# Cluster attention and two MLPs on one core: reciprocals in two tiles, and an attention loop put in another order

## The chip, the cores and the metric

The kernel runs on one core of a Trainium2 chip. The metric is the device time of one execution in microseconds. Before the change the median of three runs was 825.31 us (824.75 to 825.86).

## The reference, cut to what matters

Sixteen heads (2 batches of 8), 768 tokens, head size 64. Every query and key is given to the nearest of 16 centroids; a query sees only the keys of its own cluster. Then come two MLPs in a row.

```python
q_assign = argmax(einsum(q_n, c_n)); k_assign = argmax(einsum(k_n, c_n))   # q_n, k_n, c_n: normalised
scores = where(q_assign[:, None] == k_assign[None, :], scale * q @ k.T, -1e9)
attn = exp(scores - max(scores));  attn = attn / (sum(attn) + 1e-9)
x = attn @ v                                  # 1536 tokens x 512 (8 heads x 64)
h = x @ w_in;    x = (h * sigmoid(1.702 h)) @ w_out                 # 2048 wide
g = x @ w_gate;  out = (g * sigmoid(g) * (x @ w_val)) @ w_out2      # 1536 wide
```

Inputs are float32; the weights arrive as 8-byte numbers and are decoded on the chip to float32.

## The kernel before

**Attention.** A loop over 16 heads. The work of head h in the loop has two parts. In the score part, twelve steps (six key blocks of 128, two query halves of 384) run the scores of head h on TensorE (`st`, two matmuls each, L688), and beside each step one product for the row maxima of head h+1 (`smax`, L637). ACT turns each `st` into `p` by an exponential (L698); DVE reduces each `smax` to `nm` (L642). Three PSUM banks hold `st`, so a step can run only three ahead of the exponentials. In the value part `values(h, 0)` to `values(h, 5)` (L742) multiply `p` by `v`. Three of the six blocks of `p` are first split into a high part `ph` (a cast, L705) and a low part `pl` (a subtraction on POOL, L709); five tiles hold `p`. After `values(h, 0)` TensorE turns the maxima into a row (`mrow`), ACT casts it and SP sends it into head h+1's query tile (`q<-row`, L672), which that head's scores need.

**Beside the value part.** ACT and DVE prepare head h+4: `hi_q`, `hi_k` (casts, L441 to L446) and `lo_q`, `lo_k` (subtractions, L450, L456). In odd heads `similar` multiplies queries and keys of heads h+3 and h+4 by the centroids (`sims`, L553) and `largest` finds the best centroid on DVE; in even heads `assign` writes the clusters into the query and key tiles of the next two heads. Six weight blocks are decoded during heads 3 to 8 (`take_in`: two ACT reads, then `joined` and `signed` on DVE, L284 and L289).

**The denominators.** `values` also sums `p` (a column of ones in `v`). `moved(h, n)` copies half n of the result out of PSUM on ACT: for even heads into the tile `xf` with its sums, for odd heads the result into `xf` and the sums' row into a tile `r` (L764). SP sends the sums of a pair of heads to DRAM (`sums`), fetches them spread over the lanes (`rc`), DVE inverts them (`invert`, L779), SP sends them back (`recips`) and fetches them broadcast into the same tile `r` (`r<-recips`, L787), and POOL multiplies `xf` by `r` (`norm_pair`, L792). There is one `r` tile. For the pair of heads 2p and 2p+1, `invert`, `send_recips`, `load_recips` and `norm_pair` all run in head 2p+3. At the end of that same head the next pair's sums are copied into `r`.

**Heads 0 and 1** use another form; `norm(0)` and `norm(1)` (L818 to L820) divide on DVE and free the PSUM bank of `pv`, of which there are two. `norm(1)` stands behind `assign` and `lo_q`, `lo_k` in head 2.

**MLPs.** A planner (`Plan`) lists tasks with an engine, a nominal duration and dependences, and emits them engine by engine in the order of their latest start. `AFTER` is how long it takes a result of an engine to be usable; for SP it stands for a transfer's landing. The work is cut into 28 units: 0 to 7 and 8 to 15 are the first MLP for the two batches, 16 to 27 the second. `DECODES[k]` is how many blocks of the second MLP's weights are decoded beside unit k.

Of the kernel before, what the change touches and what calls it, by code (L numbers as in the profile page):

```python
# [55 lines left out]
class Plan:  # L56
# [6 lines left out]

    AFTER = {"PE": 210.0, "ACT": 80.0, "DVE": 70.0, "POOL": 120.0, "SP": 2200.0}
    SPARE = 120.0
# [119 lines left out]
def tile_cluster_attention_two_mlps(ctx: ExitStack, tc: tile.TileContext, qk, v, cen, w1, w2, wg, wv, w3, out):  # L185
# [116 lines left out]
    def new_a():  # L302
        return dec_p.tile([128, 512], F32, tag="a", name="a")
# [6 lines left out]

    def take_in():

        while True:
            it = items[started[0]]
            fetch_to(started[0] + 1)
            started[0] += 1
            raw = raw_t.pop(it)
            a, t = new_a(), new_t()
            small(a, raw)
            low_bits(t, raw)  # L320
            fetch_to(started[0] + 2)
            yield
            joined(t, a)
            yield
            w = new_wo()
            signed(w, a, t)
            keep(it, w)
            yield

    taking = take_in()  # L330

    def take(n):
        for _ in range(n):
            next(taking, None)

# [130 lines left out]
    load_qk(3)  # L466
    zeros = acst.tile([128, NB], F32R, name="zeros")

# [515 lines left out]
    def beside_block(h, c):  # L984
        if c == 4:
            v_split(h + 1)
        if c == 5:
            moved(h, 0)
        last = h - 1
        if last > 1:  # L990
            if c == 2:
                send_sums(last)
            if last % 2 and c == 4:
                load_sums(last // 2)
        if h % 2 and h > 4:
            hp = (h - 3) // 2
            for at, step in ((0, invert), (0, send_recips), (2, load_recips), (3, norm_pair)):
                if c == at:
                    step(hp)

    for h in range(NH):
# [38 lines left out]
        for c in range(SC) if more else ():  # L1040
# [8 lines left out]
            if c == 0:  # L1049
                load_v(h + 1)  # L1050
                if ahead:
                    if h > 0:
                        if h % 2:
                            hi_k(h + 4)
                        lo_q(h + 4, nc.gpsimd if h == 1 else nc.vector)
                        lo_k(h + 4, nc.gpsimd if h == 1 else nc.vector)
                    if h + 6 < NH:
                        load_qk(h + 6)
# [18 lines left out]
            if h == 1:  # L1077
# [5 lines left out]
                if c == 4:  # L1083
                    do(largest([4, 5], sims + similar([5], ps_s, "s")))
            if h == 2 and c == 0:
                norm(1)
            take(takes.get((h, c), 0))
# [4 lines left out]
            if h % 2 and c == 2 and ahead and h > 1:  # L1092
                do(largest([h + 3, h + 4], similar([h + 3, h + 4], ps_s, "s")))
            if h == 3 and c in (3, 4):
                to_x(0, c - 3)
    send_sums(NH - 2)
    for steps_left in more_steps.values():
# [333 lines left out]
    last_x = rings["xf"].held[1]  # L1431
    for j in range(KC - 2):
        for t0, _ in parts:
            last_x.parts[j, t0] = ([], [])
# [103 lines left out]
    def last_lows():  # L1538
        for c in range(SPLIT):
            by = ("ACT", act(S)) if c == 1 else ("POOL", 1200)  # L1540
            t = p.task(
                *by, lambda c=c: p_high(NH - 1, c, nc.scalar.copy if c == 1 else nc.gpsimd.tensor_copy),
                (), (), exp_tasks[2 * c:2 * c + 2],
            )
            lows.append(p.task("POOL", 1850, lambda c=c: p_low(NH - 1, c), (), (), [t]))
# [25 lines left out]
    def plan_norm(hp, first):  # L1571
        send = p.task("SP", 1000, lambda: (send_sums(NH - 1), load_sums(hp)), (), (), first) if first else None
        turned = p.task("DVE", 350, lambda: invert(hp), (), (), [send] if send else [])
        back = p.task("SP", 1000, lambda: (send_recips(hp), load_recips(hp)), (), (), [turned])
        return p.task(
            "POOL", 1850, lambda: norm_pair(hp), (), [(last_x, (hp % (H // 2), t0)) for t0, _ in parts], [back],
        )

    to_last = [plan_norm(NH // 2 - 2, None), *out_of]
    plan_norm(NH // 2 - 1, out_of)  # L1580
# [77 lines left out]
```

## Time and profile before

| | |
|---|---|
| median of 3 runs | 825.31 us |
| the profiled execution's own time | 825.79 us |
| its span | 823.9 us |
| TensorE busy | 792.8 us (96%) |
| DVE busy | 679.8 us (83%) |
| ACT busy | 513.4 us (62%) |
| POOL busy | 163.9 us (20%) |
| mean granted TensorE clock | 0.981 |

The shares are means over two different stages: attention, up to about 276 us, and the MLPs. The view of waits names for each engine what ended its idle time. The view of windows gives, for each chosen stretch, its length, the busy time of TensorE (and the number of its instructions), of its weight loads (PEld), of DVE, ACT and POOL, then the mean granted clock, the DMA share and GB/s; cut at the first score matmul of each head it gives one row per head.

### The profile page before, as it was taken

The numbers are of one execution on the slowest core, as the hardware profiler recorded it, in microseconds if no ns is written. First come the engines' busy times: TensorE is split into PE (matmuls) and PEld (weight loads), VectorE is DVE, ScalarE is ACT, GpSimd is POOL, SyncE is SP. The second block draws the span as 40 slices with busy tenths as digits, with TensorE's granted clock in tenths as the row PEclk, the third lists the DMA queues.
The fourth block names the chain that finished last, engine by engine and source line by source line (L and its number), as shares of the span: only waits on it lengthen the run. The fifth ranks groups of instructions, "written<-read, shape, count | busy, mean of one in ns | idle before, by whom it ended". The sixth has DMA issues, their size and how long they took to land.

```text
span 823.9 us, 11806 instructions
## 1 busy us (share of the span) xinstructions
PE 792.8 (96%) x4154; PEld 694.0 (84%) x4154; DVE 679.8 (83%) x1224; ACT 513.4 (62%) x881; POOL 163.9 (20%) x155
## 2 busy tenths in 40 slices
PE   8997997898998999999999999999999999999998
PEld 6985676677766789899899999999999999999996
DVE  7885886886887679999999989999877897877753
ACT  7855876785765688788767767666434554443432
POOL 8563434565456600001000000000000000000000
PEclk9998998998998999999999999999999999999999
DMA  5121341311111448778446778464222113321202
GB/s 131 27 83 34 94 132 41 96 47 50 45 24 48 146 132 250 262 239 285 143 152 207 242 263 273 142 215 155 90 78 77 62 42 103 128 63 66 77 1 77
DMA packets 51343, 99.32 MB, mean 121 GB/s; under 512 B 19346, under 2 KB 24806, under 8 KB 51284
## 3 DMA queue, kind: packets, MB, share of 16 engines
q1 hardware_dynamic: 51060, 98.23, 37.6%
q8 instruction: 33, 0.54, 0.3%
q10 hardware_dynamic: 224, 0.33, 0.1%
q14 instruction: 26, 0.21, 0.1%
HBM read 76.75 MB, written 21.06 MB: 119 GB/s over the span
## 4 chain that ended last, share of the span: by engine, by line
PE 70%; DVE 16%; ACT 6%; DMA 3%; issue 3%; POOL 1%; SPq 1%; ACTq 0%; DVEq 0%; POOLq 0%
PE h L384 28%; PE a L384 20%; PE pv L742 8%; PE st L688 7%; PE smax L637 3%; DMA r<-recips 2%; PE pv L801 2%; DVE b L379 2%; DVE t L284 1%; DVE c L1264 1%; DVE wd L289 1%; ACT p L698 1%; DVE g L379 1%; DVE xs L345 1%; DVE s L1208 1%
## 5 line engine op out<-in xcount | busy, mean ns | idle before, releaser
L384 PE MATMUL h<-xc,b 128*128 128x384 f32 x1680 | 317.8, 337 | 1.3 <-DVE c L1264 0.6
L384 PEld LDWEIGHTS h<-xc,b 128*128 128x128 f32 x1680 | 291.6, 188 | 11.8 <-DVE u L1264 2.2
L384 PE MATMUL a<-g,sp 128*128 128x512 f32 (+1 forms) x768 | 144.3, 336 | 0.0
L384 PEld LDWEIGHTS a<-g,sp 128*128 128x128 f32 x768 | 124.9, 188 | 16.9
L642 DVE TENSOR_REDUCE nm<-smax 128x1 f32<-128x384 f32 x192 | 98.6, 553 | 33.5 <-PE smax L637 32.8
L688 PE MATMUL st<-q,k 128*128 128x384 f32 (+1 forms) x384 | 105.4, 367 | 14.6 <-ACT p L698 13.7
L384 PE MATMUL a<-sp,g 128*128 128x512 f32 x432 | 109.6, 393 | 0.0
L698 ACT ACTIVATE p<-st 128x384 f32<-128x384 f32 x192 | 87.1, 491 | 26.0 <-PE st L688 22.3
L688 PEld LDWEIGHTS st<-q,k 128*128 128x128 f32 (+1 forms) x384 | 74.2, 206 | 21.8 <-ACT p L698 20.2
L384 PEld LDWEIGHTS a<-sp,g 128*128 128x128 f32 x432 | 80.2, 188 | 13.2
L376 ACT CAST b<-s 128x512 fp32r<-128x512 f32 x80 | 49.4, 619 | 55.4 <-PE h L384 49.3
L709 POOL TENSOR_TENSOR pl<-p,ph 128x768 fp32r<-128x768 f32 x42 | 77.1, 1843 | 13.1 <-ACT ph L705 10.9
L742 PE MATMUL pv<-p,v 128*65 128x384 f32 x168 | 63.8, 498 | 5.5 <-DVE r L820 5.5
L637 PE MATMUL smax<-k,q 80*128 80x384 f32 x192 | 66.8, 365 | 1.3 <-DVE nm L642 0.9
L1264 DVE TENSOR_TENSOR u<-h,p 128x384 f32<-128x384 f32 x80 | 44.1, 551 | 26.0 <-PE h L384 25.8
L278 ACT ACTIVATE a<-raw 128x512 f32<-128x512 f32 x68 | 45.7, 671 | 26.9 <-DVE wo L289 15.0
L379 DVE TENSOR_TENSOR b<-s,b 128x512 fp32r<-128x512 f32 x80 | 54.6, 684 | 3.7 <-ACT b L376 2.6
L379 DVE TENSOR_TENSOR g<-c,g 128x768 fp32r<-128x768 f32 x56 | 52.1, 952 | 1.7 <-ACT g L376 0.9
L376 ACT CAST g<-c 128x768 fp32r<-128x768 f32 x56 | 44.5, 833 | 11.6 <-DVE c L1279 11.3
L284 DVE SCALAR_TENSOR_TENSOR t<-a,t 128x512 int32<-128x512 int32 x68 | 46.3, 686 | 3.6 <-ACT t L281 3.5
L1272 ACT ACTIVATE c<-c 128x768 f32<-128x768 f32 (+1 forms) x56 | 38.0, 682 | 17.0 <-DVE c L1264 16.6
L376 ACT CAST b<-w 128x768 fp32r<-128x768 f32 x35 | 29.2, 835 | 31.1 <-PE h L384 29.2
(147 smaller groups left out, 1062.5 us busy)
## 6 DMA issues: line engine op xcount, KB each, us to landing
raw<-in_w SPq DMA_DIRECT2D x44, 512.0 KB, 4.6
w<-scr SPq DMA_DIRECT2D x31, 512.0 KB, 3.4
raw<-in_wg SPq DMA_DIRECT2D x12, 512.0 KB, 4.5
raw<-in_wv SPq DMA_DIRECT2D x12, 512.0 KB
w<-scrg SPq DMA_DIRECT2D x12, 512.0 KB, 3.5
w<-scrv SPq DMA_DIRECT2D x12, 512.0 KB, 3.4
st<-in_qk SPq DMA_DIRECT2D x31, 192.0 KB, 3.8
scr<-wd SPq DMA_DIRECT2D x21, 256.0 KB, 6.0
```

The lines of the kernel that those rows point to most:

```text
L278: nc.scalar.activation(a, raw[:, :, 1].bitcast(F32), ACTF.Copy, scale=2.0**-112)
L284: nc.vector.scalar_tensor_tensor(out=t, in0=a.bitcast(I32), scalar=3, in1=t, op0=ALU.logical_shift_left, op1=ALU.bitwise_or)
L376: nc.scalar.copy(to, of)
L379: eng.tensor_tensor(out=to, in0=of, in1=hi.bitcast(F32), op=ALU.subtract)
L384: nc.tensor.matmul(out=out_ps, lhsT=lhs[a], rhs=rhs[b], start=(start and j == 0), stop=(stop and j == 2), skip_group_check=True, **kw)
L637: nc.tensor.matmul(out=ps, lhsT=q2(h)[0:ONE + NC, 1, c * 128:(c + 1) * 128], rhs=k2(h)[0:ONE + NC, 1, n * HALF:(n + 1) * HALF],)
L642: nc.vector.tensor_reduce(out=nm_t[h][:, c, n:n + 1], in_=ps, axis=AX.X, op=ALU.max)
L688: nc.tensor.matmul(out=ps, lhsT=k2(h)[0:rows, a, c * 128:(c + 1) * 128], rhs=q2(h)[0:rows, a, at], start=(a == 0), stop=(a == 1),)
L698: nc.scalar.activation(p_t[h, c][:, n * HALF:(n + 1) * HALF], ps, ACTF.Exp, scale=scale)
L709: nc.gpsimd.tensor_tensor(out=pl_t[h, c], in0=p_t[h, c], in1=ph_t[h, c].bitcast(F32), op=ALU.subtract)
L742: nc.tensor.matmul(out=ps[0:m, 0:HALF], lhsT=w, rhs=x, start=(c == 3), stop=(c == 2 and j == 2), skip_group_check=True,)
L1264: lambda: nc.vector.tensor_tensor(out=to.tile[:, part], in0=ps.tile[:, 0:HALF], in1=other.tile, op=ALU.add),
```

## The change

- Two `r` tiles in turn instead of one (the second in memory freed by taking the warm-up's `zeros` from a query tile not yet in use).
- A pair's transfers are spread. For heads 2p and 2p+1: each head's sums are sent right after its last copy; both are fetched in head 2p+3, inverted there at block 4 and sent at block 5; `r` is fetched in head 2p+4; `norm_pair` runs in head 2p+5, on DVE, behind `largest`. Before, all of this from the inversion on was in head 2p+3, with `norm_pair` on POOL. The last three pairs (10/11 to 14/15) are multiplied on POOL and planned with the MLPs; before, the last two were.
- `v` is fetched two heads ahead, queries and keys are cast five heads ahead.
- `sims` and `largest` of odd heads (from head 5) stand ahead of `values(h, 0)`.
- `ph` of block 1 is cast after step 4 and of block 2 after step 8, both on ACT (block 2 was on POOL).
- `norm(1)` stands ahead of head 3's `mneg`.
- The six early blocks are decoded in heads 5 to 10, two at a time; `DECODES` gives none to units 0 to 7 and four to each of units 8 to 15; SP's `AFTER` is 4000 for 2200.

```diff
-    AFTER = {"PE": 210.0, "ACT": 80.0, "DVE": 70.0, "POOL": 120.0, "SP": 2200.0}
+    AFTER = {"PE": 210.0, "ACT": 80.0, "DVE": 70.0, "POOL": 120.0, "SP": 4000.0}
-    DECODES = (3, 1, 0, 0, 1, 0, 1, 2) + (3, 3, 4, 4, 4, 4, 3, 3)
+    DECODES = (0, 0, 0, 0, 0, 0, 0, 0) + (4, 4, 4, 4, 4, 4, 4, 4)
+    r_tile = in_turn((lambda: r_p[1], 1), (lambda: r_p[0], 1))
     def new_r():
-        return r_p.tile([128, S], F32, tag="r", name="r")
+        return r_tile([128, S], F32, "r")
-    zeros = acst.tile([128, NB], F32R, name="zeros")
+    zeros = q2_t[NQK - 1][:, 0, 0:NB]
-        if i == 6:
-            p_high(h, 1, nc.scalar.copy)
-            p_low(h, 1)
-        if i == 7:
-            p_high(h, 2, nc.gpsimd.tensor_copy)
-            p_low(h, 2)
+        if i in (4, 8):
+            p_high(h, i // 4, nc.scalar.copy)
+            p_low(h, i // 4)
-    takes = {(h, c): n for h in range(3, 9) for c, n in (((1, 1), (2, 2), (4, 1)) if h % 2 else ((1, 1), (3, 1)))}
+    takes = {}
+    for h in range(5, 5 + EARLY_ITEMS, 2):
+        takes.update({(h, 0): (0, 0), (h, 1): (1, 2), (h, 3): (1,), (h + 1, 4): (2,)})
@@ beside_block
-        last = h - 1
-        if last > 1:
-            if c == 2:
-                send_sums(last)
-            if last % 2 and c == 4:
-                load_sums(last // 2)
         if h % 2 and h > 4:
-            hp = (h - 3) // 2
-            for at, step in ((0, invert), (0, send_recips), (2, load_recips), (3, norm_pair)):
+            for at, step in ((4, invert), (5, send_recips)):
                 if c == at:
-                    step(hp)
+                    step((h - 3) // 2)
+            if c == 0 and h > 6:
+                norm_pair((h - 5) // 2, nc.vector)
+        if h % 2 == 0 and h > 5:
+            if c == 1:
+                load_recips((h - 4) // 2)
@@ the loop over heads
             moved(h - 1, 1)
+            send_sums(h - 1)
+            if h % 2 and 4 < h < NH - 1:
+                load_sums((h - 3) // 2)
+        if h == 2:
+            norm(1)
         if 1 < h < NH - 1:
             mneg(h + 1)
+            if h % 2 and ahead and h > 3:
+                do(largest([h + 3, h + 4], similar([h + 3, h + 4], ps_s, "s")))
+            for part in takes.get((h, 0), ()):
+                take(part)
             values(h, 0)
             mrow(h + 1)
-        if ahead and h > 0:
-            hi_q(h + 4)
-            if h % 2 == 0:
-                hi_k(h + 4)
+        if h > 1 and h + 2 < NH:
+            load_v(h + 2)
+        if h + 6 < NH and h > 1:
+            load_qk(h + 6)
+        casts = [] if not h else [h + 4] if h < 3 else [7, 8] if h == 3 else [h + 5] if h + 5 < NH else []
+        if casts and h != 1:
+            hi_q(casts[0])
+            hi_k(casts[0])
...
@@ last pairs
-    to_last = [plan_norm(NH // 2 - 2, None), *out_of]
+    to_last = [plan_norm(NH // 2 - 3, []), plan_norm(NH // 2 - 2, []), *out_of]
```

**How it moves instructions.** POOL from the low parts of head 5 to those of head 6, before; `ph`, `pl` are parts of `p`, `vh`, `vl` of `v`:

```order
L705 CAST ph<-p 128x768
L709 TENSOR_TENSOR pl<-p,ph 128x768 x2
L705 CAST ph<-p 128x768
L709 TENSOR_TENSOR pl<-p,ph 128x768
L792 TENSOR_TENSOR xf<-xf,r 128x768
L713 CAST vh_189<-v_186 128x3x64
```

The same place after:

```order
L706 CAST ph<-p 128x768
L710 TENSOR_TENSOR pl<-p,ph 128x768 x3
L714 CAST vh_192<-v_189 128x3x64
```

The multiplication by `r` and one cast per head have left POOL.

DVE in head 7, from the last maxima on, before (`rc` are the sums of a pair, `T`, `U` and `mx` belong to `largest`, `t` and `wo` to the decoding):

```order
L653 TENSOR_REDUCE nr<-nm 128x6
L779 TENSOR_SCALAR rc<-rc 128x12
L780 RECIPROCAL rc<-rc 128x12
L450 TENSOR_TENSOR q_1_184<-st_196,q_1_184 64x768
L456 TENSOR_TENSOR k_1_185<-st_196,k_1_185 64x768
L284 SCALAR_TENSOR_TENSOR t<-a,t 128x512
L289 SCALAR_TENSOR_TENSOR wo<-a,t 128x512
L577 STREAM_TRANSPOSE T<-sims 128x384
```

After, from the end of `largest` on:

```order
L593 TENSOR_TENSOR T<-T,wd 128x384
L790 TENSOR_TENSOR xf<-xf,r 128x768
L286 SCALAR_TENSOR_TENSOR t<-a,t 128x512
L291 SCALAR_TENSOR_TENSOR wo<-a,t 128x512
L451 TENSOR_TENSOR q_2_179<-st_196,q_2_179 64x768
L457 TENSOR_TENSOR k_2_180<-st_196,k_2_180 64x768
L286 SCALAR_TENSOR_TENSOR t<-a,t 128x512
L777 TENSOR_SCALAR rc<-rc 128x12
L778 RECIPROCAL rc<-rc 128x12
L643 TENSOR_REDUCE nm<-smax 128x1 x12
```

`largest` now comes first, the multiplication by `r` follows it, and the inversion has gone from the front of the row to its end.

DVE in head 2 (`rd` and `r` are `norm(1)`), before:

```order
L642 TENSOR_REDUCE nm<-smax 128x1 x12
L653 TENSOR_REDUCE nr<-nm 128x6
L601 TENSOR_REDUCE mx_941<-T 128x24
L603 TENSOR_TENSOR T<-T,mx_941 128x384
L606 TENSOR_SCALAR T<-T,s_246,s_247 128x384
L610 STREAM_TRANSPOSE oT<-T 64x384 x2
L450 TENSOR_TENSOR q_1_184<-st_195,q_1_184 64x768
L456 TENSOR_TENSOR k_1_185<-st_195,k_1_185 64x768
L818 TENSOR_SCALAR rd<-pv 128x6
L819 RECIPROCAL rd<-rd 128x6
L820 TENSOR_TENSOR r<-pv,rd 128x6x64
```

And after:

```order
L643 TENSOR_REDUCE nm<-smax 128x1 x12
L816 TENSOR_SCALAR rd<-pv 128x6
L817 RECIPROCAL rd<-rd 128x6
L818 TENSOR_TENSOR r<-pv,rd 128x6x64
L654 TENSOR_REDUCE nr<-nm 128x6
```

`norm(1)` has moved past the whole of `assign` and the two subtractions, to stand ahead of `nr`, from which the row of maxima is made.

## Rows read from the trace of the kernel before

**Rows 1.** The page: its first line.
```profile
span 823.9 us, 11806 instructions
```

**Rows 2.** Windows: heads 2, 3, 4, 6, 9, 13; sum of heads 2 to 14.
```profile
52.20:74.63 22.43, 16.79 (x69) 11.34 (x69) 14.35 (x26) 11.73 (x20) 8.01 (x7) 0.85 0.23 69
74.63:90.97 16.34, 16.03 (x82) 12.42 (x82) 11.82 (x21) 13.23 (x25) 8.36 (x7) 1.00 0.27 83
90.97:105.14 14.17, 13.94 (x68) 10.30 (x68) 13.62 (x25) 13.02 (x24) 7.07 (x5) 1.00 0.16 45
...
121.84:143.09 21.25, 16.20 (x68) 12.90 (x68) 13.62 (x24) 13.57 (x24) 9.76 (x8) 0.84 0.18 55
...
176.65:192.34 15.69, 15.38 (x77) 11.76 (x77) 12.88 (x26) 11.30 (x21) 7.94 (x7) 1.00 0.46 115
...
242.58:256.94 14.36, 13.98 (x69) 10.31 (x68) 13.39 (x20) 8.88 (x20) 8.51 (x7) 1.00 0.34 92
...
sum 223.92, PE 201.23 PEld 152.46 DVE 175.39 ACT 156.07 POOL 114.43; mean PE 15.48 PEld 11.73 DVE 13.49 ACT 12.01 POOL 8.80
```

**Rows 3.** Waits of PE, first 300 us: total, times, longest.
```profile
PE st L688 <- ACT p L698: 13.7, 6, 5.1
PE pv L742 <- DVE r L820: 5.5, 1, 5.5
PE sims L553 <- DVE k L456: 1.7, 6, 0.4
```

**Rows 4.** The chain that ended last, heads 5 to 6: start, length, what.
```profile
118.94 5.80 DMA r<-recips
...
125.77 1.81 POOL xf L792
...
127.60 0.48 ACT r L764
...
128.64 1.01 PE st L688 x2
```

**Rows 5.** Timeline of DVE, head 2: start, length.
```profile
66.34 0.15 DVE L818 TENSOR_SCALAR rd<-pv 128x6 f32<-128x6 f32 x1
...
66.75 0.56 DVE L820 TENSOR_TENSOR r<-pv,rd 128x384 f32<-128x384 f32 x1
```

**Rows 6.** Windows: head 4's value part; head 9's score part and value part.
```profile
98.08:105.14 7.06, 7.06 (x32) 4.12 (x31) 6.85 (x11) 6.66 (x11) 2.88 (x3) 1.00 0.05 10
176.65:183.41 6.76, 6.63 (x38) 6.28 (x38) 6.00 (x12) 5.83 (x13) 4.98 (x5) 1.00 0.47 122
183.41:192.34 8.93, 8.75 (x41) 5.49 (x40) 6.88 (x15) 5.47 (x9) 2.96 (x3) 1.00 0.45 110
```

**Rows 7.** DVE by line and shape, heads 2 to 14: busy, mean ns.
```profile
L289 DVE SCALAR_TENSOR_TENSOR wo<-a,t 128x512 int32<-128x512 int32 x6 | 4.4, 738 | 0.2
...
L590 DVE TENSOR_TENSOR T<-T,mx 128x384 f32<-128x384 f32 x6 | 3.3, 558 | 0.2
L379 DVE TENSOR_TENSOR xc<-xf,xc 128x768 fp32r<-128x768 f32 x3 | 2.9, 955 | 3.9 <-ACT xc L376 3.9
```

**Rows 8.** Timeline, heads 4 and 5.
```profile
99.22 1.82 POOL L709 TENSOR_TENSOR pl<-p,ph 128x768 fp32r<-128x768 f32 x1
...
99.53 1.93 DVE L603 TENSOR_TENSOR T<-T,mx 128x384 f32<-128x384 f32 x1
...
108.11 0.35 POOL L713 CAST vh<-v 128x192 fp32r<-128x192 f32 x1 [7.08 <-DMA v<-in_v]
```

**Rows 9.** Timeline of ACT, head 3: the cast of `ph`.
```profile
78.94 0.84 ACT L705 CAST ph<-p 128x768 fp32r<-128x768 f32 x1
```

**Rows 10.** Windows: the MLPs in three stretches.
```profile
300.00:440.00 140.00, 139.20 (x787) 128.48 (x786) 137.02 (x241) 110.84 (x191) 2.43 (x1) 1.00 0.69 224
440.00:580.00 140.00, 139.84 (x794) 130.60 (x793) 131.59 (x231) 96.48 (x160) 0.00 (x0) 1.00 0.63 212
580.00:820.00 240.00, 240.00 (x1236) 220.05 (x1235) 182.41 (x325) 98.00 (x156) 0.00 (x0) 1.00 0.21 71
```

More of the change, by code (lines that the diff above doesn't have):

```diff
@@ L309, in new_wo, with take @@
         return wo_p.tile([128, 512], F32, tag="wo", name="wo")
[L311 to L316, printed above, removed]
+    taken = {}
+    def take(part):
+        n = started[part]
+        it = items[n]
+        started[part] += 1
+        if part == 0:
+            fetch_to(n + 1)
             raw = raw_t.pop(it)
-            a, t = new_a(), new_t()
+            a, t = taken[n] = new_a(), new_t()
             small(a, raw)
             low_bits(t, raw)
-            fetch_to(started[0] + 2)
-            yield
+            fetch_to(n + 3)
+        elif part == 1:
+            a, t = taken[n]
             joined(t, a)
-            yield
+        else:
+            a, t = taken.pop(n)
             w = new_wo()
@@ L327, in take_in @@
             keep(it, w)
[L328 to L334, printed above, removed]
     ctx.enter_context(
@@ L1049, in tile_cluster_attention_two_mlps @@
             if c == 0:
-                load_v(h + 1)
-                if ahead:
[L1052 to L1058, printed above, removed]
+                if h < 2:
+                    load_v(h + 1)
+                    if h:
+                        load_v(h + 2)
+                        hi_k(casts[0])
+                    for i in casts:
+                        lo_q(i, nc.gpsimd)
+                        lo_k(i, nc.gpsimd)
+                    load_qk(h + 6)
+                if ahead:
                     if h + 5 == NH:
@@ L1084, in tile_cluster_attention_two_mlps @@
                     do(largest([4, 5], sims + similar([5], ps_s, "s")))
-            if h == 2 and c == 0:
-                norm(1)
-            take(takes.get((h, c), 0))
+            for part in takes.get((h, c), ()) if c else ():
+                take(part)
+            if h > 1 and c == 1:
+                for i in casts[:1]:
+                    lo_q(i)
+                    lo_k(i)
             for n in beside_values.get((h, c), ()):
@@ L1091, in tile_cluster_attention_two_mlps @@
                 fetch_to(2)
-            if h % 2 and c == 2 and ahead and h > 1:
-                do(largest([h + 3, h + 4], similar([h + 3, h + 4], ps_s, "s")))
+            if h == 3 and c == 4:
+                do(largest([6, 7], similar([6, 7], ps_s, "s")))
+                hi_q(8)
+                hi_k(8)
+            if h == 4 and c == 2:
+                lo_q(8)
+                lo_k(8)
             if h == 3 and c in (3, 4):
                 to_x(0, c - 3)
-    send_sums(NH - 2)
     for steps_left in more_steps.values():
@@ L1431, in tile_cluster_attention_two_mlps @@
     last_x = rings["xf"].held[1]
-    for j in range(KC - 2):
+    for j in range(KC - 3):
         for t0, _ in parts:
@@ L1539, in last_lows @@
         for c in range(SPLIT):
-            by = ("ACT", act(S)) if c == 1 else ("POOL", 1200)
+            by = ("ACT", act(S)) if c else ("POOL", 850)
             t = p.task(
-                *by, lambda c=c: p_high(NH - 1, c, nc.scalar.copy if c == 1 else nc.gpsimd.tensor_copy),
+                *by, lambda c=c: p_high(NH - 1, c, nc.scalar.copy if c else nc.gpsimd.tensor_copy),
                 (), (), exp_tasks[2 * c:2 * c + 2],
@@ L1571, in plan_norm @@
     def plan_norm(hp, first):
-        send = p.task("SP", 1000, lambda: (send_sums(NH - 1), load_sums(hp)), (), (), first) if first else None
-        turned = p.task("DVE", 350, lambda: invert(hp), (), (), [send] if send else [])
-        back = p.task("SP", 1000, lambda: (send_recips(hp), load_recips(hp)), (), (), [turned])
+        if hp > NH // 2 - 3:
+            if first:
+                first = [p.task("SP", 1000, lambda: send_sums(NH - 1), (), (), first)]
+            got = p.task("SP", 1000, lambda: load_sums(hp), (), (), first)
+            turned = p.task("DVE", 350, lambda: invert(hp), (), (), [got])
+            first = [p.task("SP", 1000, lambda: (send_recips(hp), load_recips(hp)), (), (), [turned])]
         return p.task(
-            "POOL", 1850, lambda: norm_pair(hp), (), [(last_x, (hp % (H // 2), t0)) for t0, _ in parts], [back],
+            "POOL", 1850, lambda: norm_pair(hp), (), [(last_x, (hp % (H // 2), t0)) for t0, _ in parts], first,
         )
-    to_last = [plan_norm(NH // 2 - 2, None), *out_of]
+    to_last = [plan_norm(NH // 2 - 3, []), plan_norm(NH // 2 - 2, []), *out_of]
     plan_norm(NH // 2 - 1, out_of)
```

9 lines of the change are left out of this document (6 added, 3 removed).

## The prediction, made before the changed kernel had run

> **What bounds the kernel now.** I read the page's first line, then the view of windows, first by stage and then by head, then the waits of TensorE, and last the chain that ended last around one such wait. The profiled execution took 825.79 us, of which the span is 823.9 us [rows 1]; what lies around the span, 1.89 us, stays. The median of the runs is 825.31 us, 0.48 us lower, so I sum on 825.79 and take 0.48 off at the end.
>
> From 300 us on TensorE is the bound: in the three stretches of the MLPs it is busy 139.20 of 140, 139.84 of 140 and 240.00 of 240 us [rows 10]. Nothing is to be won there. Heads 2 to 14 are different: they take 223.92 us, in which TensorE is busy 201.23 [rows 2], and some of that busy time ran at half clock. Head 4 takes 14.17 us at granted clock 1.00, head 6, which has the same work, 21.25 us at 0.84; head 2 takes 22.43 us at 0.85 [rows 2]. Odd heads that also multiply by the centroids take 15.69 us where nothing disturbs them (head 9) [rows 2].
>
> What disturbs them is named by the waits: `st` waits 13.7 us in all for the exponentials (6 times, up to 5.1), and `pv` once 5.5 us for `norm(1)` [rows 3]. The chain before the longest of these shows why [rows 4]: `r` takes 5.80 us to come back from DRAM, POOL then multiplies for 1.81 us, then ACT copies a row of sums into `r` (0.48 us), and only then come the exponentials and the score matmul at 128.64. The copy has to wait because there is one `r` tile and POOL is still reading the pair before. ACT works in order, so the exponentials of head 6 queue behind the copy. Around such a wait the clock is granted at the lower of its two levels, 1.2 of 2.4 GHz, for a part of the head, which is how the mean comes to 0.84 in head 6. So a wait of about 5 us costs 7: 21.25 less 14.17 is 7.08.
>
> **The change part by part.**
>
> *Two `r` tiles, `norm_pair` two heads later.* The copy in head 2p+3 goes into the other tile. That tile was last read by the multiplication of pair p-1, which now stands in the same head on DVE, behind `largest`. The multiplication ends some 12 us after the head's start: 6.76 us of scores [rows 6], half a microsecond for the last maximum, seven operations of `largest` at about 0.56 [rows 7], and its own 0.96. The copy comes at some 14.5 us, as it needs five of the six groups of values: 6.76, 1.87 for `sims` (8.93 less 7.06) and five sixths of 7.06 [rows 6]. So this wait goes, and the half clock with it. The transfers now have a head each, over 13 us against a landing of 5.80 us at worst [rows 4], so they are late nowhere. The price is 0.96 us of DVE (the nearest row is a two-input operation on the same 128x768, 955 ns) [rows 7]. Heads 7, 9, 11 and 13 have that on DVE, and heads 5, 7 and 9 one more decoding step (0.74 us) [rows 7]. Head 9 has DVE busy 12.88 of 15.69 us [rows 2], so 14.6 afterwards, still less than the head. What hides it is TensorE's value part; should it stop doing so, it costs at most 0.96 us in four heads.
>
> *The `norm(1)` of head 2.* It moves ahead of `nr`, so the 5.5 us wait goes. In its place `nr`, and with it the row of maxima, comes later by `norm(1)`'s own length: from 66.34 to 66.75 + 0.56, that is 0.97 us [rows 5]. TensorE waits that long for `mrow`, from nothing (if the last maximum leaves DVE early) to 0.97; I take 0.97.
>
> *`sims` first.* The same matmuls, moved ahead of the values. Their inputs were cast a head earlier, so the wait for the low part of `k`, 1.7 us in 6 times [rows 3], goes. New is that their PSUM banks are those of `st`: the first must wait for the exponential of step 9. That is between nothing and one step, 0.56 us (6.76 / 12) [rows 6]; I take nothing beyond what the value below leaves for it.
>
> *`v` two heads ahead.* POOL sat 7.08 us until `v` landed and began `vh` only after the head had begun [rows 8]; its three subtractions then ended late. They end earlier now, which frees the tiles of `p` that step 10 of the same head waits for.
>
> *`ph` on ACT.* One cast of 0.84 us [rows 9] per head moves from POOL to ACT, into the score part, where ACT is busy 5.83 of 6.76 us [rows 6]: 6.67 of 6.76. That fits, barely. Ends: nothing, or the full 0.84 us in 13 heads, 10.9 us. I take nothing, since the casts stand after steps 4 and 8, each with room for the three PSUM banks to run ahead, where one cast stood before at step 6 and cost part of a step anyway.
>
> *Weight decoding.* Units 8 to 15 get 32 blocks for 28, and 0 to 7 none for 8. A block is two DVE operations of about 0.7 us (the one shown is 738 ns) [rows 7]. Four blocks more in 440 to 580 us are 5.9 us at most: DVE goes from 131.59 to 137.5 of 140, which is what it has now in 300 to 440 (137.02), where TensorE loses 0.80 us against 0.16 [rows 10]. So this costs up to 0.6 us, and the first stretch, 11.8 us lighter on DVE, gives back up to 0.8. The new landing time for SP only reorders. I take 0.5 us for both, between a gain of 0.8 and a loss of 3.
>
> **The sum.** An even head is 14.17 us at most (head 4) [rows 2]. Its parts at their cleanest are 6.76 us (a score part with no long wait, of head 9) and 7.06 us (the value part of head 4) [rows 6], 13.82 together. I take 14.0, between these, for heads 4, 6, 8, 10, 12, 14 and for 13, which has no `sims` either. An odd head with `sims` took 6.76 + 8.93 = 15.69 us [rows 6] including some 0.4 us of the wait for `k`; I take 15.4 for heads 5, 7, 9 and 11. Head 3 stays at 16.34 [rows 2]. Head 2 is 14.17 + 0.97 = 15.14. Together 7 x 14.0 + 4 x 15.4 + 16.34 + 15.14 = 191.1 us for 223.92, a gain of 32.8. Then 825.79 - 32.8 + 0.5 - 0.48 = 793.0 us. With every head at its cleanest (13.82, and 15.3) it would be 1.7 us less, and without the 0.97 us and with the first MLP stretch clean 789.0; with 14.17 and 15.69 it is 795.4.
>
> **The rivals.**
>
> *ACT becomes the bound of the score part.* For it: 6.67 of 6.76 us leaves nothing for the copies of the head before, which fall into the same part. Against it: busy times in a part paced by TensorE contain the latency of each exponential, not only the time until the next can start. Half of the 0.84 us in 13 heads, 5.5 us, gives 798.5; all of it 803.9.
>
> *POOL and DVE hold each other up.* A comparison on DVE of 128x384 takes 558 ns where `largest` does it [rows 7], and 1.93 us where `assign` does it at 99.53, while POOL is at a `pl` from 99.22 to 101.04 [rows 8]. If the four multiplications and the subtractions beside them wait so for a `pl` of 1.82 us, four odd heads lose up to 1.8 us each: 7.2 us, 800.2. Against it: `pl` now ends, by my count, some 8 us into the head and the multiplication begins after 11. Beside this row stands the Trainium skill, Perfetto Trace Analysis, section Optimizing Scalar/DVE Operations: GPSIMD and DVE share a read port of SBUF, so moving work from one to the other may not help. It speaks against this very move; the row agrees that such waits exist, and by the rule the four multiplications would be dear whenever POOL reads at that time.
>
> *The `r` tile is still waited for.* If DVE's multiplication slips behind the copy (a margin of about 2.5 us), ACT waits again in heads 5 to 13. With half of the gain of those heads lost (223.92 less 191.1, without head 2's 7.3, is 25.5) it is 805.8. The margin speaks against it, since the wait would have to be longer than in any row for DVE.
>
> *Slower: the decoding starves TensorE.* In units 8 to 15 each block's two DVE operations stand in one row with the sums that release TensorE's PSUM banks. If the planner's new order puts the blocks ahead of them and none of the 32 is hidden, 32 x 1.48 = 47 us are added in these units: 793.0 + 47 = 840. It decides against the change from 32 us on, that is when TensorE's busy share between 410 and 550 us falls below 81% (139.84 of 140 + 32). Against it: 28 blocks stand there now at 139.84 of 140 us [rows 10].
>
> **How the numbers follow.** The forecast of 793.0 us with its own range of 789 to 797 has a chance of 0.72. ACT as the bound 0.14, POOL and DVE 0.05, the `r` tile 0.06, starved MLPs 0.03. The range that should hold 8 in 10 takes the forecast's and the nearer half of ACT's: 788.5 to 800.5. A measurement of this kernel can tell about 0.2% (1.7 us) from no change. All cases but the last are faster by more; of the last I give two thirds to slower. Faster 0.96, same 0.02, slower 0.02.
>
> **What would show it.** Right: in the waits of TensorE the lines for the exponentials and for `norm(1)` fall from 19.2 us to under 3, ACT's copy into `r` waits for nobody, the granted clock is 1.00 in all heads, even heads take 13.8 to 14.2 us, and the MLPs are as long as before (within 1 us). Wrong: a score part over 7 us with ACT busy throughout (first rival), long `xf` or `q` operations on DVE beside a `pl` (second), a wait of ACT for DVE's `xf` (third), TensorE under 99% in units 8 to 15 (fourth). A wait for the row of maxima at the start of heads 6 and 8, where two fetches of 512 KB now stand ahead of it on SP's queue, would be one I have left out.

## The result, and the profile after

The changed kernel takes 789.86 us (median of 4 runs, 788.83 to 790.90), the kernel before 825.19 us on the same chip (4 runs): a ratio of 0.9571 (95% interval 0.9555 to 0.9588). The profiled execution took 788.83 us with a span of 787.0 us. A second profile of the same kernel (changed_again, below) gives heads 2 to 14 in 189.27 us where the first gives 189.36, and the rest in 545.57 for 545.33. Over the eight traces with the same quotas and landing time (table below) the rest spreads over 0.9 us, so half a microsecond can be read in the heads but not in the rest. The profiled execution of one kernel below (old_ph_no_norm, 948.73 us) ran at a mean granted clock of 0.753 from end to end, and that kernel's numbers are those of its other three executions.

The view of windows by head (columns as in [rows 2]): heads 2, 3, 4, 7, 8, 11, 12 and the sum of heads 2 to 14.

```profile
52.31:67.00 14.69, 14.19 (x69) 10.32 (x69) 13.08 (x26) 12.12 (x21) 7.21 (x6) 1.00 0.33 102
67.00:82.85 15.85, 15.78 (x83) 12.48 (x83) 10.28 (x19) 13.95 (x25) 7.18 (x6) 1.00 0.14 38
82.85:97.07 14.22, 13.91 (x69) 10.29 (x69) 13.48 (x25) 13.96 (x27) 7.62 (x6) 1.00 0.19 48
...
126.48:141.86 15.38, 15.31 (x77) 11.76 (x76) 13.91 (x25) 13.67 (x26) 7.21 (x6) 1.00 0.51 137
141.86:155.59 13.73, 13.63 (x69) 10.34 (x69) 12.44 (x25) 12.83 (x23) 7.64 (x6) 1.00 0.32 83
...
184.72:200.85 16.13, 15.51 (x76) 11.72 (x76) 14.02 (x27) 9.70 (x21) 7.50 (x6) 1.00 0.16 44
200.85:214.44 13.59, 13.59 (x68) 10.34 (x68) 10.86 (x20) 11.06 (x22) 7.64 (x6) 1.00 0.14 33
...
sum 189.36, PE 187.45 PEld 142.25 DVE 165.96 ACT 161.38 POOL 98.20; mean PE 14.42 PEld 10.94 DVE 12.77 ACT 12.41 POOL 7.55
```

These heads took 223.92 us before [rows 2], so 34.6 us went here. Of it 13.8 us is TensorE's busy time (201.23 to 187.45) and 20.8 us is its idle time (22.7 to 1.9). Of the busy time 11.8 us went in the five heads 2, 6, 8, 10 and 14, whose granted clock had been 0.82 to 0.90; it is now 1.00 in every head.

TensorE's waits from 60 us to the end (columns as in [rows 3]):

```profile
PE smax L638 <- DVE nm L643: 0.6, 1, 0.6
PE h L384 <- DVE c L1285: 0.3, 1, 0.3
PE mrow L670 <- DVE nr L654: 0.3, 1, 0.3
PE st L689 <- ACT p L699: 0.2, 1, 0.2
```

Of the 13.7 and 5.5 us of [rows 3] 0.2 us is left. The largest wait is a new one, for the first maxima of head 11, and the row of maxima of head 2 is waited for 0.3 us.

The other 2.45 us (1.7 to 2.6 over the eight traces) came from the stage behind head 14. One window from the start of head 15 to the end, first of the kernel before, then of the changed one:

```profile
276.12:823.90 547.78, 542.98 (x2935) 498.65 (x2934) 462.80 (x813) 321.65 (x537) 12.16 (x9) 1.00 0.45 149
```

```profile
241.67:787.00 545.33, 541.41 (x2935) 498.62 (x2934) 463.34 (x813) 322.65 (x538) 12.19 (x7) 1.00 0.45 149
```

The number of instructions is the same; 0.88 us of the gain is TensorE's idle time and 1.57 us its busy time. Split at the same instruction of TensorE, about the 800th, first before, then changed:

```profile
276.12:421.96 145.84, 144.71 (x804) 131.02 (x804) 131.18 (x227) 113.32 (x198) 12.16 (x9) 1.00 0.66 213
```

```profile
241.67:385.27 143.60, 143.27 (x804) 131.01 (x804) 129.79 (x222) 106.89 (x186) 12.19 (x7) 1.00 0.59 186
```

So 2.24 us are won up to there, and what follows takes 401.73 us for 401.94. Last, the timeline of DVE and of POOL from the middle of head 7 (which starts at 126.48) into head 8 (141.86):

```profile
134.88 0.36 DVE L581 TENSOR_TENSOR T<-T 128x192 f32<-128x192 f32 x1
...
137.82 0.95 DVE L790 TENSOR_TENSOR xf<-xf,r 128x768 f32<-128x768 f32 x1
...
142.68 0.17 DVE L777 TENSOR_SCALAR rc<-rc 128x12 f32<-128x12 f32 x1
142.88 0.23 DVE L778 RECIPROCAL rc<-rc 128x12 f32<-128x12 f32 x1
143.02 3.77 DVE L643 TENSOR_REDUCE nm<-smax 128x1 f32<-128x384 f32 x8
...
132.90 1.85 POOL L710 TENSOR_TENSOR pl<-p,ph 128x768 fp32r<-128x768 f32 x1 [0.22 <-ACT ph L706]
...
135.11 0.60 POOL L715 TENSOR_TENSOR vl<-v,vh 128x192 fp32r<-128x192 f32 x1
143.49 0.83 POOL L706 CAST ph<-p 128x768 fp32r<-128x768 f32 x1 [7.78 <-ACT p L699]
```

The two engines nearly take turns. POOL's third low part ends at 134.75, 0.13 us before DVE's first addition of `largest`; POOL is through with `v` at 135.71, two microseconds before DVE multiplies; and DVE's last operation on SBUF ends at 143.11, 0.38 us before POOL begins again. The experiments show that this order in time carries a good part of the gain.

### The profile page after: what moved, and what is told of

Same layout as the page of the kernel before. It is cut to its first block, busy times and chain, and to the rows that moved or that the text cites. A ratio compares the mean times of both kernels' runs of the same rounds, so it can differ in the third digit from the quotient of the medians.

```text
span 787.0 us, 11774 instructions
## 1 busy us (share of the span) xinstructions
PE 777.6 (99%) x4154; PEld 683.8 (87%) x4154; DVE 671.0 (85%) x1228; ACT 519.7 (66%) x895; POOL 147.7 (19%) x137
## 4 chain that ended last, share of the span: by engine, by line
PE 89%; DVE 5%; ACT 4%; issue 1%; DVEq 0%; ACTq 0%
PE h L384 35%; PE a L384 29%; PE pv L740 11%; PE st L689 7%; PE smax L638 3%; PE pv L799 2%; ACT p L699 2%; PE sims L554 1%; ACT ph L706 1%; DVE nm L643 1%; DVE b L379 1%; PE warm L474 0%; DVE s L1229 0%; ACT q L442 0%; DVE wo L291 0%
## 5 line engine op out<-in xcount | busy, mean ns | idle before, releaser
L689 PE MATMUL st<-q,k 128*128 128x384 f32 (+1 forms) x384 | 98.0, 345 | 1.0 <-ACT p L699 0.2
L699 ACT ACTIVATE p<-st 128x384 f32<-128x384 f32 x192 | 84.4, 492 | 18.2 <-PE st L689 16.4
L689 PEld LDWEIGHTS st<-q,k 128*128 128x128 f32 (+1 forms) x384 | 68.2, 190 | 8.0 <-ACT p L699 6.1
L638 PE MATMUL smax<-k,q 80*128 80x384 f32 x192 | 62.8, 344 | 1.1 <-DVE nm L643 0.6
L740 PE MATMUL pv<-p,v 128*65 128x384 f32 x168 | 61.9, 485 | 0.0
L376 ACT CAST g<-c 128x768 fp32r<-128x768 f32 x56 | 45.3, 835 | 12.2 <-DVE c L1300 11.8
```

Of the source, the lines that this page charges most:

```text
L376: nc.scalar.copy(to, of)
L638: nc.tensor.matmul(out=ps, lhsT=q2(h)[0:ONE + NC, 1, c * 128:(c + 1) * 128], rhs=k2(h)[0:ONE + NC, 1, n * HALF:(n + 1) * HALF],)
L689: nc.tensor.matmul(out=ps, lhsT=k2(h)[0:rows, a, c * 128:(c + 1) * 128], rhs=q2(h)[0:rows, a, at], start=(a == 0), stop=(a == 1),)
L699: nc.scalar.activation(p_t[h, c][:, n * HALF:(n + 1) * HALF], ps, ACTF.Exp, scale=scale)
L740: nc.tensor.matmul(out=ps[0:m, 0:HALF], lhsT=w, rhs=x, start=(c == 3), stop=(c == 2 and j == 2), skip_group_check=True,)
```

## Experiments

The table puts all of them beside each other. "Heads" is the sum of heads 2 to 14, "rest" the time from the start of head 15 to the end of the span, both of the profiled execution. Each ratio is to the kernel before run beside it (medians from 823.15 to 825.19 us).

| kernel | median (range), us | ratio to before (95%) | heads | rest |
|---|---|---|---|---|
| before | 825.19 (824.75 to 825.86) | | 223.92 | 547.78 |
| changed | 789.86 (788.83 to 790.90) | 0.9571 (0.9555 to 0.9588) | 189.36 | 545.33 |
| changed_again | 789.21 (788.82 to 790.01) | 0.9571 (0.9544 to 0.9598) | 189.27 | 545.57 |
| two_r_only | 811.39 (807.46 to 813.10) | 0.9841 (0.9809 to 0.9874) | 205.51 | 547.85 |
| two_r_norm1 | 806.52 (800.57 to 807.41) | 0.9791 (0.9768 to 0.9813) | 197.89 | 548.49 |
| old_quotas | 791.85 (791.24 to 792.31) | 0.9611 (0.9592 to 0.9629) | 189.15 | 548.58 |
| old_landing | 790.85 (789.83 to 791.69) | 0.9598 (0.9579 to 0.9618) | 189.02 | 546.56 |
| norm_on_pool | 791.48 (790.91 to 792.02) | 0.9605 (0.9566 to 0.9643) | 191.89 | 545.94 |
| old_ph | 801.20 (800.78 to 803.10) | 0.9727 (0.9686 to 0.9768) | 203.00 | 545.23 |
| sims_late | 802.16 (796.97 to 805.91) | 0.9738 (0.9668 to 0.9808) | 200.34 | 545.35 |
| v_one_ahead | 793.44 (792.34 to 795.51) | 0.9631 (0.9590 to 0.9673) | 195.43 | 545.92 |
| old_ph_no_norm | 791.91 (791.82 to 791.97) | 0.9601 (0.9570 to 0.9633) | | |
| ph_both_late | 797.10 (796.51 to 797.54) | 0.9664 (0.9637 to 0.9691) | 196.29 | 546.11 |
| x0_later | 788.27 (787.70 to 789.38) | 0.9560 (0.9536 to 0.9584) | 188.31 | 545.87 |

### The r tile alone: two_r_only

The kernel before with

```diff
-    r_p = pool(ctx, "r", 1)
+    r_p = [pool(ctx, "r0", 1)]
...
+    r_tile = in_turn((lambda: r_p[1], 1), (lambda: r_p[0], 1))
...
-        return r_p.tile([128, S], F32, tag="r", name="r")
+        return r_tile([128, S], F32, "r")
...
+    r_p.append(pool(att, "r1", 1))
...
-    zeros = acst.tile([128, NB], F32R, name="zeros")
+    zeros = q2_t[NQK - 1][:, 0, 0:NB]
```

> The kernel before with two r tiles in turn (and zeros in a query tile, which makes the room), all else in its old order: the multiplication by r stays on POOL in head 2p+3, behind the transfers. Theory (one r tile makes ACT's copy, and behind it the exponentials, wait): TensorE's waits for p fall from 13.7 us to under 2, the granted clock is 1.00 from head 3 on, head 6 takes 14.2 us for 21.25, and of the 26 us that heads 3 to 14 lost against the changed kernel at least 20 are won: 800 to 805 us. Rival (POOL's row): the multiplication still stands up to 5.8 us at the front of POOL's row, ahead of ph and pl of the next head; TensorE then waits for pl in place of p, at least half of the loss stays, and the time is 812 us or more.

811.39 us. Heads 3 to 14 fall from 201.49 to 184.16 us, by 17.3 of the 26.8 us that the whole change wins in them. This trace is of the shortest of four executions (807.46 us); by the medians the second tile is worth 12.1 us (823.48, the kernel before beside it, less 811.39). TensorE's wait for `p` at `st` falls from 13.7 to 0.5 us (with 1.8 us at `pv` instead). So the theory names a large part, but the rest stays, and neither number that was expected came (800 to 805; 812 or more). Head 6 and head 12 from the windows, and ACT's wait for POOL between 60 and 260 us:

```profile
120.82:136.99 16.17, 14.35 (x68) 10.18 (x68) 15.59 (x24) 12.57 (x23) 10.12 (x8) 1.00 0.25 80
...
212.81:229.56 16.75, 15.19 (x68) 11.89 (x68) 12.82 (x20) 10.16 (x20) 10.96 (x8) 0.90 0.03 6
```

```profile
ACT p L701 <- POOL pl L712: 4.6, 4, 3.2
```

The rival was right that POOL's row is a cause of its own: the multiplication waits for its transfer at the front of that row, the low parts come late, and the exponential of step 10 gets no tile (the lines are under two_r_norm1).

### With norm(1) moved as well: two_r_norm1

```diff
+        if h == 2:
+            norm(1)
         if 1 < h < NH - 1:
             mneg(h + 1)
...
-            if h == 2 and c == 0:
-                norm(1)
```

> The kernel before with two r tiles and with norm(1) ahead of head 3's row of maxima, all else as before. The difference to two_r_only prices norm(1). Theory (the 5.5 us wait and the half clock it brings are one loss): head 2 takes 14.7 us for 22.43, so 7 to 7.7 us less than two_r_only. Rival (the half clock in head 2 has another cause, the way out of heads 0 and 1): only the wait itself goes, 4.5 to 5.5 us less, and head 2 still shows a granted clock under 0.95.

Head 2 takes 14.68 us at a granted clock of 1.00, where two_r_only has 21.35 at 0.92: the wait and the half clock are one loss, as the theory said. In the two traces the heads differ by 7.62 us, the medians by 4.9 (the profiled execution was the shortest of five); what the other four lost elsewhere is open. The trace also shows what the rest of the change has to remove. First head 6 (POOL, then ACT), then head 12 (DVE, POOL, and TensorE's wait):

```profile
117.74 1.83 POOL L795 TENSOR_TENSOR xf<-xf,r 128x768 f32<-128x768 f32 x1 [9.55 <-DMA r<-recips]
...
123.23 0.87 ACT L701 ACTIVATE p<-st 128x384 f32<-128x384 f32 x2 [3.00 <-POOL pl L712]
...
205.13 2.60 DVE L347 TENSOR_TENSOR xs<-xf 128x768 f32<-128x768 f32 x1
...
205.01 1.91 POOL L795 TENSOR_TENSOR xf<-xf,r 128x768 f32<-128x768 f32 x1 [5.53 <-DMA r<-recips]
...
209.32 0.44 PE L640 MATMUL smax<-k,q 80*128 80x384 f32 x1 [1.76 <-DVE nm L645]
```

In head 6 a late transfer becomes a late low part. In head 12 there is another effect: DVE's subtraction takes 2.60 us (0.93 in the changed kernel) while POOL multiplies beside it, the maxima queue behind it, TensorE waits 1.76 us and runs at a mean granted clock of 0.90 in that head.

### The planner's numbers: old_quotas and old_landing

```diff
-    DECODES = (0, 0, 0, 0, 0, 0, 0, 0) + (4, 4, 4, 4, 4, 4, 4, 4)
+    DECODES = (3, 1, 0, 0, 1, 0, 1, 2) + (3, 3, 4, 4, 4, 4, 3, 3)
```

> The changed kernel with DECODES of before. Theory (the MLPs are 2.45 us shorter because units 0 to 7 no longer decode): the 2.2 us are given back in units 0 to 7, 791.8 to 792.3 us, with TensorE's three waits there back. Rival (SP's landing time of 4000 in the planner did it): no change, 789.6 to 790.2 us. Third: what stands at the border of the two stages did it: no change here nor with the old landing time.

```diff
-    AFTER = {"PE": 210.0, "ACT": 80.0, "DVE": 70.0, "POOL": 120.0, "SP": 4000.0}
+    AFTER = {"PE": 210.0, "ACT": 80.0, "DVE": 70.0, "POOL": 120.0, "SP": 2200.0}
```

> The changed kernel with SP's AFTER at 2200 as before. Theory (quotas): no change, 789.6 to 790.2 us. Rival (landing time): 791.8 to 792.3 us. Third: no change.

With the old quotas the rest takes 548.58 us, 3.25 more than in the changed kernel (2.5 to 3.4 over the eight traces), and TensorE waits in the first units again, 2.2 us in three places for DVE (in the kernel before 0.9 us in three places, one of them for ACT; in the changed kernel 0.3 us in one):

```profile
PE h L384 <- DVE c L1285: 2.2, 3, 1.6
```

So the quotas give the gain. Of the 3.25 us 1.9 is idle time and 1.4 busy time of TensorE. The old landing time gives 546.56 us; the eight traces with the new quotas and landing time (table) lie between 545.23 and 546.11, so it may cost a few tenths, which these runs do not settle. The ratios agree: that of old_quotas lies above the changed kernel's interval (though it touches the wider one of changed_again), that of old_landing overlaps it.

### One part of the attention loop taken back at a time

norm_on_pool:

```diff
-                norm_pair((h - 5) // 2, nc.vector)
+                norm_pair((h - 5) // 2)
```

> The changed kernel with norm_pair of the four pairs in heads 7 to 13 on POOL in place of DVE, at the same place in the program (r has landed a head earlier, so POOL waits for nothing). Theory (the gain comes from the second r tile and the late place, not from the engine): POOL has room, 7.2 of 15.4 us busy, the multiplications run some 8 to 10 us into the head, TensorE waits for nothing new: 789 to 791 us. Rival (POOL's reading holds DVE up, as its xs of 2.60 us for 0.96 beside POOL's xf in two_r_norm1 suggests): largest runs beside POOL's xf, up to 1.8 us late in each of four heads, the maxima of the next head wait: 792 to 797 us.

791.48 us lies between the two ranges. The heads take 2.53 us more, and it is heads 8 and 10 that lose (15.14 and 15.12 us for 13.73 and 13.78). The rival is right in the place it named, and costs less than it said. DVE and POOL in head 7, TensorE in head 8:

```profile
134.43 1.86 DVE L581 TENSOR_TENSOR T<-T 128x192 f32<-128x192 f32 x1
...
134.25 1.83 POOL L790 TENSOR_TENSOR xf<-xf,r 128x768 f32<-128x768 f32 x1
...
144.62 0.44 PE L638 MATMUL smax<-k,q 80*128 80x384 f32 x1 [1.13 <-DVE nm L643]
```

An addition that takes 0.36 us alone ends at 136.29, 0.21 us after POOL's multiplication has ended at 136.08: it is not slowed but held. DVE does 0.95 us less and is nevertheless later.

old_ph:

```diff
-        if i in (4, 8):
-            p_high(h, i // 4, nc.scalar.copy)
-            p_low(h, i // 4)
+        if i == 6:
+            p_high(h, 1, nc.scalar.copy)
+            p_low(h, 1)
+        if i == 7:
+            p_high(h, 2, nc.gpsimd.tensor_copy)
+            p_low(h, 2)
```

> The changed kernel with the casts of ph where they stood: block 1 on ACT after step 6, block 2 on POOL after step 7. Theory (ACT's room was what decides, and both places fit): POOL ends its low parts 0.8 to 1.7 us later in each head, still ahead of the values that need them: 789 to 791 us. Rival (POOL's low parts are what step 10 waits for, as in head 6 of two_r_norm1 with 3.00 us): the exponential of step 10 waits for pl in some of 13 heads, 0.3 to 0.8 us each: 793 to 800 us.

801.20 us, 13.6 us more in the heads. The theory fell, and the rival had the wrong wait: `st` waits 0.9 us for `p`, but `smax` 7.7 us for `nm`. Head 8 (windows), then POOL and DVE in heads 7 and 8, and TensorE's longest wait:

```profile
143.28:163.14 19.86, 16.52 (x69) 13.22 (x68) 16.82 (x26) 12.89 (x22) 8.66 (x7) 0.83 0.23 58
```

```profile
135.96 1.83 POOL L710 TENSOR_TENSOR pl<-p,ph 128x768 fp32r<-128x768 f32 x1
...
145.82 2.13 POOL L710 TENSOR_TENSOR pl<-p,ph 128x768 fp32r<-128x768 f32 x1
...
136.32 1.69 DVE L581 TENSOR_TENSOR T<-T 128x192 f32<-128x192 f32 x1
...
145.04 1.25 DVE L286 SCALAR_TENSOR_TENSOR t<-a,t 128x512 int32<-128x512 int32 x1
146.21 1.77 DVE L780 TENSOR_SCALAR rc<-rc 128x12 f32<-128x12 f32 x1
...
148.71 0.69 PE L638 MATMUL smax<-k,q 80*128 80x384 f32 x1 [3.34 <-DVE nm L643]
```

The third low part ends later, holds an operation of `largest`, and DVE's row no longer ends before POOL starts in the next head. There the rest of it is held again: an operation on 12 columns takes 1.77 us for 0.17. The first maxima are 3.34 us late, and the clock falls behind them.

old_ph_no_norm tests that this is the path:

```diff
             if c == 0 and h > 6:
-                norm_pair((h - 5) // 2, nc.vector)
+                r_t.pop((h - 5) // 2)
```

> As old_ph, but the multiplications by r of the four pairs in heads 7 to 13 are left out (the result of these pairs stays undivided), so DVE has 0.95 us less to do in each of these heads. Theory (old_ph is slow because DVE's last operations of odd heads run past the next head's start into POOL's ph and pl, where they are stretched, and the maxima come late): DVE is through before POOL starts there, t and rc take 0.69 and 0.17 us again for 1.25 and 1.77, heads 8 and 10 fall from 19.86 and 19.44 to 14 to 15.5 us, and the time is 791 to 794 us. Rival (the late low parts themselves make TensorE wait): no change beyond 1 us, 800 to 802 us.

791.91 us. Taking 0.95 us from DVE in four heads gives back 9.3 us, though POOL's casts and low parts stand where they stood in old_ph. The theory holds in the time; the lengths of `t` and `rc` and of heads 8 and 10 that it names could not be read.

ph_both_late separates the engine from the place:

```diff
-        if i in (4, 8):
-            p_high(h, i // 4, nc.scalar.copy)
-            p_low(h, i // 4)
+        if i in (6, 7):
+            p_high(h, i - 5, nc.scalar.copy)
+            p_low(h, i - 5)
```

> The changed kernel with the two casts of ph on ACT both, but after steps 6 and 7, so that only the engine of block 2 differs from old_ph, and only the place from the changed kernel. POOL's third pl then ends some 8.9 us into a head, between 8.3 (changed kernel) and 9.7 (old_ph). Theory (where pl ends decides, since DVE's largest begins at 7.8 to 8.3 us into an odd head): one operation of largest is stretched by 0.5 to 0.8 us, 790 to 795 us. Rival (the place after steps 4 and 8 is what matters, for the exponentials): TensorE waits for p, 796 us or more.

797.10 us: the rival. TensorE's waits, and the operation of `largest` that the theory had in view:

```profile
PE st L689 <- ACT p L699: 4.6, 16, 0.3
```

```profile
137.97 0.50 DVE L581 TENSOR_TENSOR T<-T 128x192 f32<-128x192 f32 x1
```

DVE is held for 0.14 us only. TensorE now waits for `p` in short pieces, and each head from 2 to 14 loses 0.2 to 0.7 us; that two casts in a row use up what the three banks of `st` let ACT fall behind fits this and is not shown apart.

sims_late:

```diff
-            if h % 2 and ahead and h > 3:
-                do(largest([h + 3, h + 4], similar([h + 3, h + 4], ps_s, "s")))
...
+            if h % 2 and ahead and h > 3 and c == 2:
+                do(largest([h + 3, h + 4], similar([h + 3, h + 4], ps_s, "s")))
```

> The changed kernel with sims and largest of odd heads from 5 on back behind the third group of values, the casts still five heads ahead. Theory as predicted (sims first removes the wait for k): TensorE's wait for k comes back, 0.3 to 0.4 us in four heads, 791 to 792 us. Rival A (the earlier casts already removed it, k is ready a head before): no wait for k, 789 to 791 us. Rival B (largest now runs into the next head's maxima): TensorE waits for nm in heads 6 to 12, 0.5 to 1.5 us each with the clock falling behind it, 793 us or more.

802.16 us, 11.0 us more in the heads: rival B, and more than it said. No wait for `k` comes back. TensorE's waits up to 300 us, then POOL and DVE in head 8, which starts at 143.31:

```profile
PE smax L638 <- DVE nm L643: 9.3, 4, 3.5
```

```profile
146.00 2.13 POOL L710 TENSOR_TENSOR pl<-p,ph 128x768 fp32r<-128x768 f32 x1
...
146.39 1.76 DVE L777 TENSOR_SCALAR rc<-rc 128x12 f32<-128x12 f32 x1
```

v_one_ahead:

```diff
-        if h > 1 and h + 2 < NH:
-            load_v(h + 2)
...
+                load_v(h + 1)
                 if h < 2:
-                    load_v(h + 1)
                     if h:
-                        load_v(h + 2)
```

> The changed kernel with v fetched one head ahead, at block 0, as before. Theory as predicted (a late v holds up POOL, whose low parts then end late and free p for step 10 late): POOL's vh waits for DMA v in some heads, pl ends up to 1 us later, and TensorE waits for p now and then: 790 to 794 us. Rival (v lands within the head even so, with POOL's row free of the multiplication): no change, 789 to 791 us.

793.44 us, 6.1 us more in the heads of a profiled execution that was the longest of four (795.51). Head 10 starts at 172.36; POOL, ACT and TensorE:

```profile
172.60 0.34 POOL L714 CAST vh<-v 128x192 fp32r<-128x192 f32 x1 [5.95 <-DMA v<-in_v]
...
172.98 2.02 ACT L699 ACTIVATE p<-st 128x384 f32<-128x384 f32 x4 [1.03 <-POOL vh L714]
...
176.21 0.44 PE L638 MATMUL smax<-k,q 80*128 80x384 f32 x1 [1.75 <-DVE nm L643]
```

In head 10 the late `v` puts POOL's work on it beside the end of DVE's row. Before that it acts in another way. POOL and DVE in head 7:

```profile
131.11 5.45 POOL L710 TENSOR_TENSOR pl<-p,ph 128x768 fp32r<-128x768 f32 x3
...
134.88 1.89 DVE L581 TENSOR_TENSOR T<-T 128x192 f32<-128x192 f32 x1
```

POOL's low parts end late, as expected (136.56, for 134.75 in the changed kernel), but what that delays is `largest`, and the first maxima of head 8 come 1.17 us late. TensorE waits 3.5 us for the maxima and 1.4 us for `p`, of which 1.22 in head 14, where ACT had itself waited 4.95 us for DVE.

### One step further: x0_later, beside changed_again

```diff
-    for at in [(10, 2), (10, 3)] + [(11, c) for c in (1, 2, 4)] + ...
+    for at in [(11, c) for c in (1, 2, 2, 3, 4)] + ...
```

> The changed kernel with the two steps of the MLP's first operand in head 10 moved to head 11 (after groups 2 and 3 of the values). Theory (DVE's xc, which waits for ACT past the end of head 10, is what makes head 11's first maxima late): the 0.6 us wait for nm goes, head 11 takes 15.4 us for 16.13, 0.7 us less than changed_again. Rival (head 11's own row on DVE, 14.0 of 16.1 us, has no room): the wait moves to head 12, no gain or up to 1 us lost.

> The changed kernel as it is, run beside the others: 788 to 791 us. Every theory expects the same; it is the reference for x0_later, and shows how far the trace of one execution repeats (heads 2 to 14 in 189.0 to 189.9 us).

The change has itself moved these steps, from heads 9 to 12 to heads 10 to 12; its list does not name that. 788.27 us beside 789.21. Head 11 in the windows of x0_later:

```profile
184.35:199.71 15.36, 15.31 (x76) 11.75 (x76) 13.87 (x26) 10.07 (x21) 7.21 (x6) 1.00 0.18 49
```

It is 0.77 us shorter than in the changed kernel, the wait for its first maxima is gone, and head 12 keeps its 13.60 us. The theory holds in the trace; in the times the ranges of the two kernels overlap, so 0.9 us is the estimate and not a sure gain.

Not taken back alone were the casts five heads ahead, the place of the six early blocks, the spread of the transfers, and the late place of the multiplication with one `r` tile. What each of them is worth is open.

## Why the prediction was right, and where its reasons were not

It summed to 793.0 us; the time is 789.86, lower by 3.1. That it came so near is in part luck: it priced at nothing or tenths several edits without which the median is 1.6 to 12.3 us higher.

**Two r tiles and the late multiplication.** Right: ACT's copy into `r` waits for nobody, the waits for `p` fall to 0.2 us and the clock is full in every head. Before, between 60 and 260 us, ACT's waits began with this line, and the changed kernel has none for `r`:

```profile
ACT r L764 <- POOL xf L792: 14.3, 4, 5.2
```

In head 9 DVE's multiplication ends at 167.88 and ACT's copy begins at 170.06, a margin of 2.2 us where about 2.5 was counted. But the prediction let these two edits carry the gain of heads 3 to 14 and priced the others as nothing or tenths. Alone the second tile gives 17.3 of 26.8 us in its best execution, and less by the medians.

**norm(1).** Right. The row of maxima was waited for 0.3 us, not the 0.97 that was taken.

**sims first.** The wrong reason. The step said that the wait for `k` goes; with `sims` back in the old place it does not return, most likely because the earlier casts have already removed it (they were not taken back alone). What the place buys is that DVE is through with `largest` before the next head: 11.0 us.

**v two heads ahead.** Worth some 4 to 6 us. The low parts do end late without it, as the step says, but what they delay in the main is DVE, and through it the next head's maxima, not a tile of `p`.

**ph on ACT at no cost.** Right, and for the reason given: four steps apart the casts cost nothing, in two steps running 7 us. That is the first rival in effect, 797.1 us against its 798.5 for half of the cast. What the step did not see is the other side: the earlier cast also ends POOL's reading before DVE's.

**POOL and DVE hold each other up.** The mechanism is real and is the main thing that the change has to avoid, but its sign was the other way: on DVE a multiplication takes 0.95 us (1.46 in head 13, beside POOL's last low part), which TensorE never waits for; on POOL the four of them make the heads 2.53 us longer, because there they hold `largest`. The Trainium skill, SBUF — State Buffer, section Who interferes with whom, says that a DVE instruction with two SBUF inputs contends with a GpSimd instruction that reads SBUF, and that the second to issue waits until the first is done. The trace agrees: the held addition in norm_on_pool ends 0.21 us after POOL's multiplication.

**Slack of the r tile, starved decoding.** Neither rival showed. The margins that mattered are others: 0.13 us between POOL's third low part and `largest` in head 7, and 0.38 us between DVE's last operation and POOL's first in head 8.

**The sum.** The heads were taken as 191.1 us and are 189.36 (1.7 less): even heads reach 13.59 to 13.78 from head 8 on, where 14.0 was taken, heads 2 and 3 are 0.45 and 0.49 us shorter, and head 11 loses 0.7. The term that was mis-sized is the decoding: +0.5 us was taken, with -0.8 as the best end, and -2.45 was measured, outside the 1 us that the signs allowed the MLPs. The step counted the idle time in 300 to 440 us as all that DVE's decodes cost TensorE. Up to the 800th instruction the idle time did fall by 0.80 us (1.13 to 0.33), but the busy time of the same number of instructions fell by 1.44 as well, at a granted clock of 1.00 in both; why is not shown. Behind it, where most of the 32 blocks stand, nothing was lost (401.73 us for 401.94). The two differences, 1.7 and 2.95, add up to 4.65 us, and the profiled execution (788.83) is 4.65 below the sum on its own scale (793.48). For the row of maxima behind the two fetches of 512 KB no wait shows in heads 6 and 8.

## What to carry to other kernels

An edit that a sum prices at nothing can be what lets another one pay. Here each of four small edits, taken back alone, costs 2.5 to 13.6 us in the heads. Together that is more than lies between two_r_norm1 and the changed kernel (8.5 us in the traces, 16.7 by the medians), since all of them keep one order in time. When the stall that a profile names is removed, look for which engine finishes closest to its next deadline, and ask who can hold it there. Of two engines that hold each other, place their work apart in time before moving it from one to the other.

## What the runs showed that was not expected

How long DVE is held goes by POOL's instruction, not by its own: an operation on 128x12 took 1.77 us for 0.17, one on 128x192 took 1.86 for 0.36. The maxima, which DVE reduces from PSUM, are not held: eight take 3.77 us from 143.02 in the changed kernel with POOL's `ph` and `pl` beside them, and not one of the 192 in that kernel takes over 0.56 us, nor one in old_ph. POOL is held as well: the low part in head 8 of old_ph and of sims_late takes 2.13 us where others take 1.82 to 1.85. A hold of 1.3 us in head 7 of old_ph (1.69 for 0.36) became a wait of 3.34 us and a head 8 longer by 6.1 us (19.86 for 13.73), since it pushed DVE's last operations into POOL's next work and the clock fell behind the wait.
